# One group of softmax factors for the last two head pairs, and chained products for the first two wide groups

## The chip, the cores and the metric

The kernel runs on one core of one Trainium2 chip. The metric is device microseconds of that core, from the start of the program to its end; lower is better. The engines are PE (TensorE, matmuls), DVE (VectorE), ACT (ScalarE), POOL (GpSimd) and SP (SyncE, which here only issues DMAs). Each engine works through its own list of instructions in order and waits on semaphores of the others.

## The reference

Attention with capped scores feeds a normalized, gated feed-forward layer, and that a second one. Cut to what matters:

```python
# q, k, v: (2, 12, 448, 64)
scores = cap * tanh(q @ k.T / 8 / cap)
attn = exp(scores - max) / (sum(exp(scores - max)) + 1e-09)
x = (attn @ v) -> (896, 768)
# moe: 768 -> 1536 -> 768
xn = x / sqrt(mean(x * x) + 1e-06) * rms_g
x = (silu(xn @ w_gate) * (xn @ w_val)) @ w_out
# moe2: 768 -> 2048 -> 768
h = x @ w_in
out = (max(h, 0) + alpha * min(h, 0)) @ w_out2
```

## The kernel before, in words

**Attention.** There are 12 head pairs (2 batches of 6; a pair is 128 rows of x, two heads of 64). For pair i, `qk` makes the scores in PSUM, `soft` takes tanh and exp on ACT, `pv` multiplies the exponentials with v into the bank `oo`, and `sums` multiplies them with ones to get the row sums (`us`). Divided by the sums, `oo` is x. Every fp32 value that PE multiplies at full speed is split into a high and a low part (names `wh`/`wl` for weights, `xx`, `xh`/`xl` for operands), and a product of two such values takes three matmuls: high by high, low by high, high by low. `sums` works on plain fp32 values, and each of its matmuls writes a quarter of the partitions (32 columns of PE's array): of the eight, four can work side by side.

The quotients are made once for a group of two pairs (`members`): `evac_u` copies the sums out of PSUM on DVE and sends them with two DMAs into a small tile `gt` of 64 partitions by 28; `recip` adds, inverts and splits them into `th` and `tl` (four small DVE instructions) and sends these with two DMAs as rows into `r2`. Later `norm` has PE spread the rows over 128 partitions (`rps`, one matmul) and DVE multiply them with `ee`, the copy of `oo`. All four DMAs are issued by SP. Pair 10 is a group by itself, and the last pair (11) goes another way: `sums_now` makes half-width sums, so that all 128 partitions hold them at once, and `norm_now` inverts them there (ACT, then a DVE reciprocal of 128x448) and multiplies `oo` directly, without DMA.

**The turn to the feed-forward part.** `square` and `rms_sum` (matmuls of squares with ones, L352) give the mean square of batch 1; `rms_root` (ACT) and `rms_tail` (a DVE reciprocal of 128x448) make `rstd` of it; `xnorm` scales x. Until that is there, PE works on products of batch 0, whose `rstd` was made earlier.

**The products.** The gate and value weights are taken in 6 groups g; a pair of weight tiles and the two batches form a 2x2 block product that is computed with seven products P1 to P7 (Strassen's method in Winograd's form) instead of eight. P1 = A11 B11, P2 = A12 B21, P5 = S1 T1, P6 = S2 T2, P7 = S3 T3, P4 = A22 T4, P3 = S4 B22; S and T are sums of weights and of operands. B11 and B21 are the lower and upper three blocks of batch 0; T1, T2 and T3 need batch 1. One product of one group is `product`, 18 matmuls of 448 columns into a pair of PSUM banks. The sums that give the four results are P1+P2, U2 = P1+P6, U2+P7+P5 and U2+P7+P4 and U2+P5+P3.

From group 2 on, P1, P6, P7 and P4 are accumulated one after the other in the same banks (`pa`): between two of them the partial sum is copied out. The first two groups ("early") go another way before the change: P1 starts, is copied (`first_sum`), P2 is added on top of it in the same banks; P6, P7 and P4 are accumulated in other banks (`pb`), and DVE adds P1 to what it reads of them (`u2`, `u3`, `add21`).

**What sets the order.** The program is written in order, engine by engine, without a scheduler; from the first P5 on, PE's work is a list of slots, and a table of hooks (`do(n, rank, ...)`) places the work of the other engines after slot n. A few matmuls are cut in two by hand (`cuts`): `SHORT` cuts the last 64 columns off.

Tiles come from pools with a few buffers; an allocation waits until the former user of the buffer is done. PSUM has eight banks: `ps_s` two pairs, `ps_x` a pair, `ps_o` and `ps_r` a bank each; after attention the pool `pm` takes the place of the last three.

Of the kernel before, what the change touches and what calls it, by code (L numbers as in the profile page):

```python
# [57 lines left out]
def attn_moe_kernel(ctx: ExitStack, tc: tile.TileContext, units, qk_in, v, sel, w, gvec, alpha, out):  # L58
# [206 lines left out]
    members = [[i, i + 1] for i in range(0, NPAIR - 2, 2)] + [[NPAIR - 2]]  # L265
# [8 lines left out]
    def evac_u(i):
# [7 lines left out]
        for k in range(2):  # L282
            nc.sync.dma_start(
# [1065 lines left out]
```

## Time and profile before

| | |
|---|---|
| time, median of 3 runs | 555.68 us (555.52 to 555.75) |
| the profiled execution's own time | 555.48 us |
| its span, first to last instruction | 553.7 us |
| PE busy | 548.4 us, 99% of the span |
| DVE busy | 452.2 us, 82% |
| ACT busy | 366.5 us, 66% |

The time holds the span and some 1.8 us around it (555.48 less 553.7). Shares of busy time are means over the whole program, and PE counts as busy while a matmul is in its pipeline; which engine sets the end of a stage is read from the chain and the timelines.

### The profile page before, as it was taken

What the parts mean: (1) busy time and instruction counts of PE and PEld (TensorE: products, weight loads), DVE (VectorE), ACT (ScalarE), POOL (GpSimd) and SP (SyncE); (2) the same over time, 40 slices, a digit from 0 to 9 for tenths busy, and PEclk for the clock granted to TensorE, in tenths of its full rate; (3) what the DMA queues carried; (4) which work ended last, traced back from release to release, by engine and by line L of the source; (5) the groups of instructions that cost most, each with busy time, mean ns of one, the idle gap of its engine ahead of it and who ended that gap; (6) DMA issues with size and microseconds to landing.
All of it is one profiled execution on the core that took longest, in us unless ns stands there. A gap on an engine that the chain in (4) does not pass through costs nothing.

```text
span 553.7 us, 7698 instructions
## 1 busy us (share of the span) xinstructions
PE 548.4 (99%) x3062; PEld 462.5 (84%) x3062; DVE 452.2 (82%) x514; ACT 366.5 (66%) x427; POOL 100.6 (18%) x54
## 2 busy tenths in 40 slices
PE   8999999999999999999999999999999999999997
PEld 5444544699999999999999999999999999999996
DVE  4797889899998967878898898979866899999242
ACT  7989999458356654586757554787967996467110
POOL 0034762200056431010000038101111000000000
PEclk9999999999999999999999999999999999999999
DMA  7855420400334535065510663005412257013022
GB/s 256 289 173 184 157 77 3 172 2 0 115 117 168 171 115 170 1 217 182 174 54 1 228 225 117 1 0 172 171 58 65 108 203 250 2 59 115 0 101 99
DMA packets 17180, 66.07 MB, mean 119 GB/s; under 512 B 3448, under 2 KB 5368, under 8 KB 17144
## 3 DMA queue, kind: packets, MB, share of 16 engines
q1 hardware_dynamic: 16712, 65.07, 34.3%
q8 instruction: 24, 0.39, 0.3%
q10 hardware_dynamic: 288, 0.38, 0.2%
q0 software_dynamic: 144, 0.13, 0.1%
q14 instruction: 12, 0.10, 0.1%
HBM read 62.66 MB, written 2.75 MB: 118 GB/s over the span
## 4 chain that ended last, share of the span: by engine, by line
PE 98%; ACT 1%; DVE 0%; issue 0%; DVEq 0%
PE m L407 22%; PE s L407 21%; PE m L761 11%; PE s L761 9%; PE s L735 8%; PE m L735 7%; PE oo L234 6%; PE s L205 5%; PE us L247 3%; PE s L420 1%; PE m L420 1%; ACT pt L214 1%; PE warm L431 1%; ACT pt L219 1%; PE us L257 1%; PE rps L330 1%
## 5 line engine op out<-in xcount | busy, mean ns | idle before, releaser
L131 ACT CAST wh<-wt 128x768 fp32r<-128x768 f32 x105 | 87.1, 832 | 69.4 <-PE s L761 25.0
L125 POOL TENSOR_TENSOR wt<-wt 128x768 f32<-128x768 f32 x33 | 77.2, 2348 | 263.6 <-DVE wt L117 133.7
L137 DVE TENSOR_TENSOR wl<-wt,wh 128x768 fp32r<-128x768 f32 x108 | 115.0, 1068 | 11.4 <-ACT wh L131 11.1
L112 ACT CAST top<-raw 128x768 f16<-128x768 bf16 x64 | 68.8, 1078 | 34.1 <-DVE wt L117 20.4
L407 PE MATMUL s<-xx,wh 128*128 128x448 f32 x336 | 81.3, 367 | 0.1
L407 PE MATMUL m<-xx,wh 128*128 128x448 f32 x336 | 80.2, 365 | 0.0
L117 DVE SCALAR_TENSOR_TENSOR wt<-raw,top 128x768 uint32<-128x768 uint32 x68 | 68.6, 1010 | 0.9 <-ACT top L112 0.9
L407 PEld LDWEIGHTS s<-xx,wh 128*128 128x128 f32 x336 | 63.0, 188 | 6.4 <-issue 0.9
L407 PEld LDWEIGHTS m<-xx,wh 128*128 128x128 f32 x336 | 63.1, 188 | 4.9
L625 DVE TENSOR_TENSOR xx<-b,xx 128x896 fp32r<-128x896 f32 (+1 forms) x40 | 48.7, 1226 | 0.6 <-ACT xx L638 0.6
L761 PE MATMUL m<-xx,wh 128*128 128x448 f32 x156 | 47.2, 365 | 0.0
L214 ACT ACTIVATE pt<-s,cinv 128x896 f32<-128x896 f32 (+1 forms) x48 | 41.0, 911 | 5.8 <-PE s L205 5.5
L407 PE MATMUL m<-xx,wl 128*128 128x448 f32 (+1 forms) x170 | 43.3, 364 | 0.0
L407 PE MATMUL s<-xx,wl 128*128 128x448 f32 (+1 forms) x170 | 43.3, 364 | 0.0
L761 PE MATMUL s<-xx,wh 128*128 128x448 f32 x132 | 40.4, 365 | 0.0
L234 PE MATMUL oo<-pt,vt 128*32 128x448 f32 x384 | 38.6, 540 | 0.5 <-ACT pt L219 0.4
L219 ACT ACTIVATE pt<-pt,cap_t 128x3136 f32<-128x3136 f32 (+2 forms) x13 | 35.3, 2713 | 0.4
L735 PE MATMUL m<-xx,wh 128*128 128x448 f32 x120 | 34.1, 365 | 0.0
L407 PEld LDWEIGHTS m<-xx,wl 128*128 128x128 f32 x170 | 31.9, 188 | 2.5
L407 PEld LDWEIGHTS s<-xx,wl 128*128 128x128 f32 x170 | 31.8, 188 | 2.5
L234 PEld LDWEIGHTS oo<-pt,vt 128*32 128x32 f32 x384 | 12.1, 110 | 23.8 <-issue 21.0
L625 DVE TENSOR_TENSOR b<-m,b 128x896 f32<-128x896 f32 (+1 forms) x13 | 11.8, 907 | 24.4 <-PE m L761 18.1
(187 smaller groups left out, 1018.0 us busy)
## 6 DMA issues: line engine op xcount, KB each, us to landing
raw<-w_in SPq DMA_DIRECT2D x68, 768.0 KB
rw<-qk_in SPq DMA_DIRECT2D x11, 480.0 KB
vt<-v_in SPq DMA_DIRECT2D x12, 256.0 KB
out<-b SPq DMA_DIRECT2D x2, 448.0 KB
out<-b SPq DMA_DIRECT2D x2, 224.0 KB
out<-e SPq DMA_DIRECT2D x1, 448.0 KB
out<-c SPq DMA_DIRECT2D x2, 224.0 KB
gt<-us SPq DMA_DIRECT2D x22, 3.5 KB
```

The lines of the kernel that those rows point to most:

```text
L112: copy(top_of[u].bitcast(F16)[:, 1::2], raw_t[u].bitcast(BF16)[:, 4:4 * n + 4:4])
L117: nc.vector.scalar_tensor_tensor(out=f_t[u].bitcast(U32), in0=raw_t.pop(u).bitcast(U32)[:, 1:2 * n + 1:2], scalar=13, in1=top_of.pop(u), o ...
L125: add(out=t, in0=f_t[a], in1=f_t[b], op=op)
L131: copy(h_t[u], f_t[u].rearrange("p (k m) -> p k m", m=P))
L137: nc.vector.tensor_tensor(out=l_t[u], in0=f_t[u].rearrange("p (k m) -> p k m", m=P), in1=h_t[u], op=ALU.subtract)
L214: nc.scalar.activation(out=t[:, 2 * g:2 * g + w], in_=st.pop((i, g))[:, :w, :S], func=AF.Tanh, scale=cinv)
L219: nc.scalar.activation(out=t[:, done:to], in_=t[:, done:to], func=AF.Exp, scale=cap_t)
L234: nc.tensor.matmul(oo[i][q * Q:q * Q + Q, :S], vv[:, n, q % 2 * Q:q % 2 * Q + Q], t[:, min(n, TILES - 1), :], start=c == 0, stop=c == TG, ...
L407: nc.tensor.matmul(ps[:, r, c0:c1], lhs, rhs[:, c0:c1], start=first and n == 0, stop=n == len(mm) - 1, skip_group_check=True,)
L625: nc.vector.tensor_tensor(out=out, in0=a, in1=b, op=op)
L735: nc.tensor.matmul(dst[m], wt[:, kk * MB + m, :], x, start=first and u == 0 and kk == 0 and n == 0, stop=u == 1 and kk == 1 and n == 2, sk ...
L761: nc.tensor.matmul(dst[m], wt[:, kk * MB + m, :], x, start=start and ks + kk == 0 and i == 0, stop=fin and last and kk == 1 and i == 2, sk ...
```

## The change

- **Sums.** All 12 pairs use quarter-width sums and groups of two; pairs 10 and 11 share one group. `sums_now` and `norm_now` are gone: pair 11 gets `evac_u`, a place in `recip`, and a `norm`. The second DMA of the last `evac_u` and of the last `recip` is issued by ACT instead of SP. `oo` of pair 11 is copied by ACT.
- **Squares.** The squares of pairs 10 and 11 are added on DVE (`join_squares`), so that `rms_sum` has two parts instead of three; its result goes to the bank of `ps_o`.
- **Products.** P2 of both early groups comes first and has its own banks (`pb`), then P1 in `pa`; B21 is made before B11. The early groups then use the chain P1, P6, P7, P4 in `pa` as the later groups do; P1, P2, P5, U2 and P4 of group 0 are copied by ACT (`keep_part`, `ps1`), and DVE joins. P4 of group 1 now stands ahead of P1 of group 2. `ps_x` lives on after attention, and `chain_pair` alternates between it and `pm`.
- **Around it.** T3's sum and high part and the high part of S3 of group 0 are made earlier; a silu of one column (`tiny`) draws ACT's table load ahead of T1's casts; weight buffers are assigned in another order; cuts are S/2 and there is one fewer.

The core of the diff:

```diff
     ps_s = ctx.enter_context(tc.tile_pool(name="ps_s", bufs=2, space=PSUM))
+    ps_x = ctx.enter_context(tc.tile_pool(name="ps_x", bufs=1, space=PSUM))
...
-    ps_x = att.enter_context(tc.tile_pool(name="ps_x", bufs=1, space=PSUM))
...
-        h_t[u] = wpool.tile([P, UK, P], F32R, tag="wh", name="wh", bufs=WH)[:, :k]
+        if u not in h_t:
+            h_t[u] = wpool.tile([P, UK, P], F32R, tag="wh", name="wh", bufs=WH)[:, :k]
...
-        us[i] = ps_r.tile([P, 512], F32, tag="u", name="us")
+        us[i] = ps_s.tile([P, 2, 512], F32, tag="s", name="us")[:, 0] if i == NPAIR - 1 else under()
...
-    def sums_now(i):
-        us[i] = ps_s.tile([P, 2, 512], F32, tag="s", name="us")[:, 0]
-        for n, t in enumerate(tiles_of(i)):
-            h = n % 2
-            nc.tensor.matmul(
-                us[i][h * D:h * D + D, :S], half[:, h] if n > 5 else ones[:, :D], t, start=n < 2, stop=n > 5,
-                skip_group_check=True,
-            )
...
-    members = [[i, i + 1] for i in range(0, NPAIR - 2, 2)] + [[NPAIR - 2]]
+    members = [[i, i + 1] for i in range(0, NPAIR, 2)]
...
+    def evac_u(i, queues=(nc.sync, nc.sync)):
...
-        for k in range(2):
-            nc.sync.dma_start(
+        for k, q in enumerate(queues):
+            q.dma_start(
...
-        for r0, x in ((0, th), (32, tl)):
+        for r0, x, q in zip((0, 32), (th, tl), queues):
             row = rr[r0:r0 + w].rearrange("r (p s) -> r p s", p=RP)
-            nc.sync.dma_start(out=row.bitcast(F32), in_=x[m].bitcast(F32))
+            q.dma_start(out=row.bitcast(F32), in_=x[m].bitcast(F32))
...
-    def norm_now(i):
-        b, p = divmod(i, NP)
-        u = sb.tile([P, S], F32, tag="us", name="us")
-        nc.scalar.activation(out=u, in_=us.pop(i)[:, :S], func=AF.Identity, bias=eps_t)
-        for j in (last - 3, last - 2):
-            square(j)
-        nc.vector.reciprocal(out=u, in_=u)
-        nc.vector.tensor_tensor(out=xf[b][:, p, :], in0=oo.pop(i)[:, :S], in1=u, op=ALU.mult)
-        square(i)
+    def join_squares(b):
+        x, y = s2[b].pop(), s2[b].pop()
+        nc.vector.tensor_tensor(out=x, in0=y, in1=x, op=ALU.add)
+        s2[b].append(x)
...
+        for x in ("A12", "A11"):
+            for g in range(2):
+                h_t["g", g, x], l_t["g", g, x] = (
+                    wpool.tile([P, UK, P], F32R, tag=t, name=t, bufs=WH) for t in ("wh", "wl")
+                )
...
-        a(11, xnorm, 0)
-        z(11, xnorm, 1)
+        a(11, xnorm, K3)
+        z(11, xnorm, K3 + 1)
...
-        sums_now(last)
+        sums(last)
+        evac_u(last, (nc.sync, nc.scalar))
+        for j in (last - 3, last - 2):
+            square(j)
         pv(last)
-        xnorm(2)
+        xnorm(K3 + 2)
...
-            pa[g] = pair_tile(ps_s, "s")
-        recip(len(members) - 1)
-        norm_now(last)
+            pb[g] = pair_tile(ps_s, "s")
         late = []
-        product(pa[0], ("g", 0, "A11"), "B11", True, rows=(0,))
+        evac_o(last, nc.scalar.copy)
+        w_lo(("g", 1, "A12"))
+        xnorm(0, late)
+        recip(len(members) - 1, (nc.sync, nc.scalar))
+        xnorm(1, late)
+        xnorm(2, late)
+        lows(late)
+        product(pb[0], ("g", 0, "A12"), "B21", True)
+        w_hi(("g", 0, "S1"))
+        sum4("g", 1)
+        product(pb[1], ("g", 1, "A12"), "B21", True, rows=(0,), span=range(6))
         norm(last - 1, under())
+        norm(last, third()[:, 0])
         square(last - 1)
-        product(pa[0], ("g", 0, "A11"), "B11", True, rows=(1,))
-        for m in range(NP - 3, NP):
-            xnorm(m, late)
-        lows(late)
-        rms_sum(B - 1, third()[:, 0])
+        square(last)
+        join_squares(B - 1)
+        product(pb[1], ("g", 1, "A12"), "B21", True, rows=(0,), span=range(6, 3 * K3))
+        product(pb[1], ("g", 1, "A12"), "B21", True, rows=(1,))
+        rms_sum(B - 1, upper("ms"))
         rms_keep(B - 1)
         rms_root(B - 1)
-        first_sum(0, ct("c21"))
-        w_hi(("g", 0, "S1"))
-        w_lo(("g", 1, "A12"))
-        sum4("g", 1)
+        w_lo(("g", 0, "S1"))
         rms_tail(B - 1)
-        product(pa[1], ("g", 1, "A11"), "B11", True, cuts={(0, 4): (S // 2,), (1, 4): SHORT})
-        first_sum(1, ct("c21"))
-        w_hi(("g", 1, "S1"))
-        c11 = [spare[B - 1][:, :2], xpool.tile([P, 2, S], F32, tag="B22l", name="c11")]
-        product(pa[0], ("g", 0, "A12"), "B21", False)
-        nc.scalar.copy(c11[0], pa[0][:, :, :S])
-        product(pa[1], ("g", 1, "A12"), "B21", False)
...
-        pm = ctx.enter_context(tc.tile_pool(name="pm", bufs=2, space=PSUM))
+        pm = ctx.enter_context(tc.tile_pool(name="pm", bufs=1, space=PSUM))
+        n_chain = [0]
         def chain_pair():
-            return pair_tile(pm, "m")
+            n_chain[0] += 1
+            return pair_tile(*((ps_x, "x") if n_chain[0] % 2 else (pm, "m")))
...
+        d11, ps1 = {}, {}
+        def keep_part(to, g, ps, home):
+            to[g] = home()
+            nc.scalar.copy(to[g], ps[g][:, :, :S])
+        for g in range(2):
+            keep_part(d11, g, pb, lambda: h_of(g)[:, 2:])
+            pa[g] = chain_pair()
+            product(pa[g], ("g", g, "A11"), "B11", True, cuts={} if g else {(0, 4): (S // 2,)})
+        w_hi(("g", 1, "S1"))
+        nc.scalar.activation(out=tiny, in_=cap_t, func=AF.Silu)
         i1 = (B - 1) * NP
         one, low = tile_maker("T1", i1, x0[:, lo3], x1[:, lo3], x0[:, lo3])
         for k in range(K3):
             one(k)
-        nc.scalar.copy(c11[1], pa[1][:, :, :S])
+            if k == 0:
+                w_lo(("g", 1, "S1"))
         for g in range(2):
-            w_lo(("g", g, "S1"))
+            ps1[g] = ct("p1")
+            nc.scalar.copy(ps1[g], pa[g][:, :, :S])
+        for g in range(2):
             w_hi(("g", g, "S2"))
...
-        BANKS = ({"P1": pa, "P2": pa, "P6": pb, "P7": pb, "P4": pb, "P5": pc, "P3": pc},
-                 {"P1": pa, "P6": pa, "P7": pa, "P4": pa, "P2": pb, "P5": pc, "P3": pc})
+        BANK = {"P1": pa, "P6": pa, "P7": pa, "P4": pa, "P2": pb, "P5": pc, "P3": pc}
...
-                product(BANK[p][g], (lay, g, wn), xn, first, cuts={(1, 4): SHORT} if here in PACED else {})
+                product(BANK[p][g], (lay, g, wn), xn, first, cuts={(1, 4): (S // 2,)} if here in PACED else {})
...
-        layer("g", G1, twice(("P5", "P6", "P7", "P3")) + [("P4", 0), ("P1", 2), ("P4", 1)])
+        layer("g", G1, twice(("P5", "P6", "P7", "P3", "P4")) + [("P1", 2)])
...
-            gate(1, g, 0, c11)
-            do(at_["P6"] + 1, 1, u2_first, g, None)
-            soon = g == 1
-            do(at_["P7"] + 1 - soon, 1 + 0.6 * soon, u3, g, lambda: cu("c22"))
-            do(max(at_["P7"], at_["P5"]) + 1 - soon, 1 + 0.6 * soon, add22, g)
-            gate(max(at_["P7"], at_["P5"]) + 2, g, 3, c22)
-            do(at_["P4"] + 1, 1, add21, g)
-            gate(at_["P4"] + 2, g, 2, c21)
-            do(at_["P3"] + 1, 1, add12, g)
+            do(3 + 3 * g, 1.2, join11, g)
+            do(4 + 2 * g, 1.3, silu, g, 0, d11)
+            do(5 + 2 * g, 0.95, times, g, 0, d11)
+            do(3 + g, 0.5, keep_part, c22, g, pc, lambda: cu("c22"))
+            do(at_["P6"] + 1, -1, keep_part, c12, g, pa, lambda g=g: home12(g))
+            do(at_["P7"] + 1, 1, join_part, c22, g, pa)
+            gate(at_["P7"] + 3 - g, g, 3, c22)
+            do(at_["P3"] + 1, 2.2, join_part, c12, g, pc)
             gate(at_["P3"] + 2, g, 1, c12)
+            if g == 0:
+                do(at_["P4"] + 1, -1, keep_part, c21, g, pa, lambda: ct("c21"))
+                gate(at_["P4"] + 1, g, 2, c21)
+            else:
+                gate(at_["P4"] + 1, g, 2, pa)
...
+            w_lo(("g", 0, "S2"))
+            one2(1)
+            w_lo(("g", 1, "S2"))
+            one2(2)
+            w_hi(("g", 0, "S3"))
+            tt(x1[:, lo3], x1[:, hi3], x1[:, lo3], ALU.subtract)
+            operand("T3", x1[:, lo3])
```

Where the instructions stand. PE from the sums of the last pair on, before (L257 `sums_now`, L234 `pv`, L407 `product`, L330 `norm`, L352 `rms_sum`):

```order
L257 MATMUL us<-pt,ones 64x448 x6
L257 MATMUL us<-pt,half 64x448 x2
L234 MATMUL oo<-pt,vt 32x448 x16
L407 MATMUL s<-xx,wh 128x448 x3
L407 MATMUL s<-xx,wl 128x448 x3
L407 MATMUL s<-xx,wh 128x448 x3
L330 MATMUL rps<-r_1_92,sel_t 128x448
L407 MATMUL s<-xx,wh 128x448 x3
L407 MATMUL s<-xx,wl 128x448 x3
L407 MATMUL s<-xx,wh 128x448 x3
L352 MATMUL s<-s_1033,ones 128x448
L352 MATMUL s<-sq,ones 128x448 x2
```

PE at the same place in the changed kernel (L249 `sums`, L236 `pv`, L393 `product`, L322 `norm`, L339 `rms_sum`):

```order
L236 MATMUL oo<-pt,vt 32x448 x16
L393 MATMUL s<-xx,wh 128x448 x3
L393 MATMUL s<-xx,wl 128x448 x3
L393 MATMUL s<-xx,wh 128x448 x6
L393 MATMUL s<-xx,wl 128x448 x3
L393 MATMUL s<-xx,wh 128x448 x6
L393 MATMUL s<-xx,wl 128x448 x3
L322 MATMUL rps<-r_1_93,sel_t 128x448
L322 MATMUL s<-r_1_93,sel_t 128x448
L393 MATMUL s<-xx,wh 128x448 x6
L393 MATMUL s<-xx,wl 128x448 x3
L393 MATMUL s<-xx,wh 128x448 x3
```

The two norms stand behind 24 matmuls of products instead of one norm behind 9; ahead of this piece `sums` has eight matmuls of 32 columns, and the two parts of `rms_sum` follow next. After them only the two P1 (36 matmuls) stand ahead of P5, where 54 stood before.

ACT at the same time, before (from the last exp's follower on: L131 high part of a weight, L578 the root of one column, L337 `norm_now`, L316 `square`, L385 casts of an operand, L359 `rms_root`, L576 `first_sum`):

```order
L131 CAST wh<-wt 128x768
L578 ACT_TABLE_LOAD
L578 ACTIVATE cinv<-rms_b 128x1
L337 ACTIVATE us<-us,eps_t 128x448
L316 ACTIVATE sq<-xf 128x448 x4
L385 CAST xx<-xf 128x448 x3
L359 ACTIVATE spare<-s,rms_b 128x448
L576 COPY c_1222<-s 128x896
L131 CAST wh<-wt 128x768
L576 COPY c_1250<-s 128x896
```

And in the changed kernel (L275 the DMA of `evac_u`, L264 the copy of `oo`, L372 casts, L295 the DMA of `recip`, L346 `rms_root`, L662 `keep_part`):

```order
L275 DMA gt<-us 32x1x28
L308 ACTIVATE sq<-xf 128x448 x2
L567 ACT_TABLE_LOAD
L567 ACTIVATE cinv<-rms_b 128x1
L264 COPY ee<-oo 128x448
L372 CAST xx<-xf 128x448
L295 DMA r_1_93<-tl 4x16x28
L372 CAST xx<-xf 128x448 x2
L133 CAST wh<-wt 128x768
L308 ACTIVATE sq<-xf 128x448 x2
L346 ACTIVATE spare<-ms,rms_b 128x448
L662 COPY b_1264<-s 128x896 x2
```

ACT's queue now holds two DMA issues, each behind a wait for DVE; two squares moved ahead of the table load, and two copies of a product pair stand ahead of T1's casts.

ACT at P6 and P7 of the early groups, in the changed kernel (L629 the high part of an operand, L662 `keep_part`, L133 the high part of a weight):

```order
L133 CAST wh<-wt 128x768
L629 CAST xx<-xf 128x1344
L662 COPY b_1436<-x 128x896
L133 CAST wh<-wt 128x768
L662 COPY c_1440<-s 128x896
L629 CAST xh<-xf 128x1344
L662 COPY b_1436<-m 128x896
L133 CAST wh<-wt 128x768
```

The `b` rows are the copies of U2 out of the chain's banks; P7 of the same group accumulates in these banks and follows them. Before the change, DVE read the banks there (`u2`), and ACT had no copy.

## Rows read from the trace of the kernel before

**Rows 1.** Page, part 1: span and busy time of the engines

```profile
span 553.7 us, 7698 instructions
...
PE 548.4 (99%) x3062; PEld 462.5 (84%) x3062; DVE 452.2 (82%) x514; ACT 366.5 (66%) x427; POOL 100.6 (18%) x54
```

**Rows 2.** All waits of PE for others: total us, times, longest us

```profile
PE warm L431 <- DVE ones L428: 1.1, 1, 1.1
PE oo L234 <- ACT pt L219: 0.4, 1, 0.4
```

**Rows 3.** The chain that ended last, in order of time: start us, length us, what

```profile
90.08 1.64 PE us L247 x16
...
95.12 0.20 PE rps L330
95.32 3.16 PE us L257 x16
...
103.64 0.21 PE rps L330
...
105.69 2.25 PE s L352 x6
107.94 11.04 PE s L407 x56
...
126.29 7.30 PE s L420 x36
...
133.64 7.53 PE s L407 x36
...
239.74 7.38 PE m L407 x37
```

**Rows 4.** Timeline of DVE and ACT: start us, length us, engine, instruction

```profile
91.79 0.62 DVE L280 COPY us<-us 128x448 f32<-128x448 f32 x1
...
95.37 1.28 ACT L578 ACT_TABLE_LOAD   x1
...
96.39 0.68 DVE L376 SCALAR_TENSOR_TENSOR xf<-xf,g_t,spare 128x448 f32<-128x448 f32 x1
...
96.67 0.20 ACT L578 ACTIVATE cinv<-rms_b 128x1 f32<-128x1 f32 x1
...
98.07 0.23 DVE L292 SCALAR_TENSOR_TENSOR gf<-gt,eps_t 32x28 f32<-32x28 f32 x1
...
98.88 0.18 DVE L299 TENSOR_TENSOR tl<-gf,th 32x28 fp32r<-32x28 f32 x1
...
107.81 0.95 DVE L137 TENSOR_TENSOR wl<-wt,wh 128x768 fp32r<-128x768 f32 x1
107.98 0.64 ACT L359 ACTIVATE spare<-s,rms_b 128x448 f32<-128x448 f32 x1 [1.10 <-PE s L352]
...
108.52 0.90 ACT L576 COPY c<-s 128x896 f32<-128x896 f32 x1
108.68 2.94 DVE L362 RECIPROCAL spare<-spare 128x448 f32<-128x448 f32 x1
...
112.45 0.62 DVE L625 TENSOR_TENSOR xf<-xf 128x448 f32<-128x448 f32 x1
```

**Rows 5.** Timeline at the products after attention, the same columns

```profile
128.62 1.31 ACT L638 CAST xx<-xf 128x1344 fp32r<-128x1344 f32 x1
...
132.40 1.09 DVE L625 TENSOR_TENSOR b<-s,c 128x896 f32<-128x896 f32 x1 [0.88 <-PE s L420]
```

**Rows 6.** Timeline of SP's queue, the same columns

```profile
98.91 0.66 SPq L303 DMA_DIRECT2D r<-th  x1
...
100.41 1.30 SPq L101 DMA_DIRECT2D raw<-w_in  x3
```

**Rows 7.** Windows: us, length, busy by engine, clock, DMA share, GB/s

```profile
100.20:100.40 0.20, 0.20 (x8) 0.09 (x4) 0.20 (x1) 0.00 (x0) 0.20 (x1) 1.00 0.13 18
101.20:107.80 6.60, 6.60 (x34) 4.83 (x27) 5.49 (x9) 2.81 (x5) 0.93 (x1) 1.00 0.90 357
```

More of the change, by code (lines that the diff above doesn't have):

```diff
@@ L73, in attn_moe_kernel @@
     cap_t = const.tile([P, 1], F32, name="cap_t")
+    tiny = const.tile([P, 1], F32, name="tiny")
     cinv = aconst.tile([P, 1], F32, name="cinv")
@@ L394, in attn_moe_kernel, with product @@
     fill_ps = {}
-    SHORT = (S - 64,)
-    def product(ps, u, name, first, rows=(0, 1), cuts={}):
+    def product(ps, u, name, first, rows=(0, 1), cuts={}, span=range(3 * K3)):
         wh, wl = h_t[u], l_t[u]
@@ L403, in product @@
             mm = [(a[:, r * K3 + k, :], x[:, k, :]) for a, x in ((wh, xh), (wl, xh), (wh, xl)) for k in range(K3)]
-            for n, (lhs, rhs) in enumerate(mm):
+            for n in span:
+                lhs, rhs = mm[n]
                 edges = [0, *cuts.get((r, n), ()), S]
@@ L410, in product, with products @@
                     )
-    def products(pss, us, name):
+    def products(pss, us, name, first):
         xh, xl = oper[name]
@@ L420, in products @@
                 nc.tensor.matmul(
-                    ps[:, r, :S], wt[u][:, r * K3 + k, :], x[:, k, :], start=n < len(both),
+                    ps[:, r, :S], wt[u][:, r * K3 + k, :], x[:, k, :], start=first and n < len(both),
                     stop=x is xl and k == K3 - 1, skip_group_check=True,
@@ L658, in tile_maker, with h_of @@
             return one, low
+        hb = {}
+        def h_of(g):
+            if g % 2 == 0 and g // 2 not in hb:
+                hb[g // 2] = block(g // 2)
+            return hb[g // 2][:, g % 2 * 4:g % 2 * 4 + 4, :]
+        d11, ps1 = {}, {}
[8 more added lines that the diff above has]
+        nc.scalar.activation(out=tiny, in_=cap_t, func=AF.Silu)
         i1 = (B - 1) * NP
@@ L685, in pslot @@
             early = lay == "g" and g < 2
-            BANK = BANKS[not early]
-            first = p in (("P6", "P5") if early else ("P1", "P2", "P5"))
+            first = p in ("P1", "P2", "P5")
             wn, xn = OPER[p]
@@ L693, in pe @@
                 if first and early:
-                    BANK[p][g] = chain_pair() if p == "P5" else side_pair()
+                    BANK[p][g] = side_pair()
                 elif first and p == "P1":
@@ L702, in pe @@
                     if g == 1:
-                        products([BANK[p][0], BANK[p][1]], [("g", i, wn) for i in range(2)], xn)
+                        products([BANK[p][0], BANK[p][1]], [("g", i, wn) for i in range(2)], xn, first)
                     return
-                product(BANK[p][g], (lay, g, wn), xn, first, cuts={(1, 4): SHORT} if here in PACED else {})
+                product(BANK[p][g], (lay, g, wn), xn, first, cuts={(1, 4): (S // 2,)} if here in PACED else {})
             at_of[lay, g, p] = len(slots)
@@ L829, in attn_moe_kernel @@
                     do(n - 2, 0, lambda u: w_kept(u), u)
-                else:
+                elif u != ("g", 0, "S3"):
                     do(n - 2, 0, w_hi, u)
@@ L886, in attn_moe_kernel @@
             do(0, 6, w_next, u)
-        def h_of(g):
-            if g % 2 == 0 and g // 2 not in hb:
-                hb[g // 2] = block(g // 2)
-            return hb[g // 2][:, g % 2 * 4:g % 2 * 4 + 4, :]
         def vsum(out, ps, b):
             tt(out, ps[:, :, :S], b, ALU.add)
-        def u2(g, home):
-            c12[g] = home()
-            vsum(c12[g], pb[g], c21[g])
-        def u3(g, home):
-            c22[g] = home()
-            vsum(c22[g], pb[g], c21[g])
-        d11 = {}
-        def keep_part(to, g, ps, home):
-            to[g] = home()
-            nc.scalar.copy(to[g], ps[g][:, :, :S])
         def join_part(to, g, ps):
             vsum(to[g], ps[g], to[g])
-        def add22(g):
-            vsum(c22[g], pc[g], c22[g])
-        def add21(g):
-            vsum(c21[g], pb[g], c21[g])
-        def add12(g):
-            vsum(c12[g], pc[g], c12[g])
         def silu(g, q, of):
@@ L974, in second_operands @@
             one2(0)
-            for g in range(2):
-                w_lo(("g", g, "S2"))
-            for k in range(1, K3):
-                one2(k)
+            w_lo(("g", 0, "S2"))
[5 more added lines that the diff above has]
+            operand("T3", x1[:, lo3])
             low2()
```

23 lines of the change are left out of this document (11 added, 12 removed).

## The prediction

> **What bounds the kernel now.** I read the page first: PE is busy for 548.4 of 553.7 us [rows 1]. A busy PE need not be a bound, so the second view is the list of PE's waits for other engines: 1.5 us in all, one at the start and one for the first exp [rows 2]. The third is the chain that ended last; from the first scores to the last store it is nearly all PE's own list of matmuls, and the rows here are those that the change touches [rows 3]. So PE bounds the kernel, and a change can win only what it takes off PE's list or off small gaps that the list of waits doesn't name. DVE and ACT matter where a matmul waits for them, so their timelines are the fourth view, at the turn from attention to the products and at P7 [rows 4, 5]. The sum is made against the profiled execution's 555.48 us; the median of the runs, 555.68, lies 0.2 above it. A difference under 0.2% (1.1 us) I call none.
>
> **What leaves PE's list.** Term 1, the sums of pair 11: the half-width form takes 3.16 us, the quarter-width form of all other pairs 1.64 for the same eight matmuls [rows 3]: -1.5.
>
> Term 2, `rms_sum`: three matmuls of plain fp32 (two records each) take 2.25 us [rows 3], a third of that is 0.75, and one goes: -0.75. In its place DVE adds two squares (0.62, as the subtraction of the same size [rows 4]).
>
> Term 3, one more norm: a `rps` matmul takes 0.2 [rows 3]: +0.2.
>
> Term 4, the cuts: a stretch of 36 matmuls takes 7.30 us (0.203 each), and with one `SHORT` cut, 37 records, 7.38: such a cut costs 0.08 [rows 3]. The stretch of 56 holds 54 matmuls (10.95 us), one `SHORT` and one half cut, and takes 11.04 [rows 3]: the half cut costs 0.01. Four `SHORT` and one half become four halves: -0.3. Nothing else in the number of matmuls changes.
>
> Term 5, a gap at P7: the 36 matmuls that begin at 133.64 take 7.53 instead of 7.30 [rows 3]. P7 adds into the banks of P6, and DVE reads these first, from 132.40 to 133.49 [rows 5], ending 0.15 before P7 starts. After the change ACT copies them instead, in 0.90 [rows 4] against 1.09: of the 0.23 I take -0.2 for group 0. For group 1 the copy stands fifth on ACT (below), from nothing to 0.2 of new wait; I take 0.05, nearer the end at which short overlaps on ACT count.
>
> Sum: -1.5 - 0.75 + 0.2 - 0.3 - 0.2 + 0.05 = -2.5. That makes 553.0 for a profiled execution and 553.2 as a median.
>
> **What must stay hidden for that.** Three chains of other engines end at PE, each with its own cover.
>
> *The factors.* This is the tight one. The sums still start at 95.3 [rows 3]. In the loop DVE's copy starts 1.71 after them (90.08 to 91.79) and takes 0.62 [rows 3, 4]: here it ends at 97.65. Two DMAs go out at once, from SP and ACT. DVE goes on with one `xnorm` of three steps (1.68, from 96.39 to 98.07), a weight's low part (0.95) and another scaling (0.68) [rows 4]: 100.95. The sums have 3.3 to land. From the first step of `recip` to the issue of `th` it takes 0.84 (98.07 to 98.91 [rows 4, 6]), to the end of `tl` 0.99 [rows 4]: issues at 101.8 and about 102.0. The landing isn't in the trace. Below: the packets of the `th` issued at 98.91 run from 100.2 to 100.4 [rows 7], so they are through 1.5 after issue. Above: its partner goes out behind it, after 99.57, and the norm that reads both runs at 103.64 [rows 3], so 4.0 at the most. I take 2.0, near the lower end, since after the packets only the report is left: the factors are there at 104.0. PE comes to the norms with 24 matmuls ahead of them instead of nine. The former norm ran 5.16 after the end of the sums (103.64 less 98.48), so now it is 95.3 + 1.64 + 5.16 + 15 x 0.203 = 105.1. Margin 1.1; at the upper end the factors land at 106.0, and PE waits 0.9.
>
> ACT must be at its second DMA by 102.0. In its queue stand the first DMA (through at about 98.3, with the 0.66 that an issue takes on SP [rows 6]), two squares (0.64 each, as the root of the same size), the table load of 1.28 and the root of one column, 0.20 [rows 4], then the copy of `oo` and one cast of 0.64: 102.3 without any overlap. That is about even with DVE, so `tl` goes out at 102.0 to 102.3. Behind the waiting DMA stand casts that P1 needs, and P1 starts at 109.4.
>
> *The mean square.* From the norms (0.4 for both), 12 matmuls (2.4) and 1.5 of `rms_sum` PE is through at 109.4. DVE's multiplications, ACT's squares and the join, of which `rms_sum`'s second part waits, need some 0.4 + 4 x 0.6 = 2.8 of the first 3.55. Then root to T1: from the start of the root at 107.98 to the end of the first subtraction at 113.07 it is 5.09 [rows 4], plus a cast of at most 0.64: T1's first block at 115.1. P5 stands behind 36 matmuls instead of 54, at 109.4 + 7.3 = 116.7. Margin 1.6, where it was over 5. ACT puts two copies of 0.90, a weight cast (narrower, so at most 0.90), a table load of 1.28 and 0.2 of silu between: 109.4 + 0.64 + 4.2 = 114.2, before DVE's 114.5.
>
> *The copies at P7.* P6 starts at 124.0. Group 0's last matmul is the 30th of 36, so its banks are full at 130.1; before, the reader came as soon (126.29 and 30 x 0.203 is 132.38, and DVE started at 132.40 [rows 3, 5]). ACT then has a copy (0.90), a weight cast (0.90), a copy (0.90), a cast of 1344 columns (1.31 [rows 5]) and group 1's copy (0.90): 135.0, with the 0.15 of the hand-off 135.15. P7 of group 1 is due at 131.3 + 3.65 = 134.95; hence the 0 to 0.2 of term 5.
>
> At nothing I cost: ACT's copies of P1, P5 and P4 and DVE's joins (their banks are used again 7 us later or more; without that cover each would cost its 0.9 to 1.1), T3 and S3 made earlier (behind T2's blocks, ahead of P7 by 2 us), the alternate use of `ps_x` and `pm` (two pairs in turn, as before), and P4 of group 1 ahead of P1 of group 2. DVE loses the reciprocal of `norm_now`, of the size of the 2.94 one [rows 4]. The three raw weight loads stand behind `th` on SP and go out at 102.5 instead of 100.41 [rows 6]; what reads them comes with the later groups, some 25 us on. They matter in another way, as a rival.
>
> **A rule against it.** The row: a table load on ACT starts at 95.37 and takes 1.28, and the root behind it starts at 96.67, 0.02 after its end [rows 4]. The Trainium skill (ScalarE: Activation LUTs, section What ACT_TABLE_LOAD costs) states that a switch of tables costs about 2.66 us, the load and a drain of 1.38. By this rule ACT would come to its second DMA at 103.6, the factors would land at 105.6, and the sum would be 0.5 higher. This trace shows no such drain, so the row decides.
>
> **Rivals.**
> 1. *The factors land late.* The raw loads keep the DMA engines busy from 101.2 to 107.8 [rows 7]; now issued at 102.5 they can run into the `tl` of 102.0 to 102.3. For it: nothing keeps the two apart. Against: `tl` is ahead by a little. At the upper landing of 4.0 PE waits 0.9 to 1.2: 554.2.
> 2. *The slower side: the factors land behind the whole of the three loads.* Issued 2.1 later, the loads would be through at 109.9 [rows 6, 7], and PE would wait 4.8: 558.0. It decides from a landing after 108.7, a wait of 3.6 (556.8). Against it: in the loop such DMAs share the engines with loads, and PE has no wait there [rows 2].
> 3. *ACT is late at P7* by half a microsecond, since its copies stand in order behind a cast that DVE delays: 553.7.
> 4. *T1 late*: the margin of 1.6 used up by a late join or a long ACT queue, and a wait of up to 1: 554.2.
> 5. *The change doesn't do what it says*: the last quarter-width sums don't run side by side; term 1 falls away: 554.7.
> 6. *ACT stops for 1.4 at the table load* ahead of its second DMA, as in the rule above: 553.7.
>
> **How the numbers follow.** Likeliest, 0.66: 553.2, by itself 552.6 to 553.7. Its lower end has no wait at P7, the runs' own 0.2 and some 0.3 for gaps under a tenth that these rows don't resolve. Rival 1: 0.13, of it 0.04 above 554.57, where the difference falls under 0.2%. Rival 2: 0.05. Rival 3: 0.08. Rival 4: 0.04. Rivals 5 and 6: 0.02 each. Faster: 0.66 + 0.09 + 0.08 + 0.04 + 0.02 = 0.89. Within 0.2%: 0.04 + 0.02 = 0.06. Slower: 0.05. The range goes from 552.5 to 554.4, which takes in rivals 3 and 6 and most of 1 and 4.
>
> **What would show it.** Right: a list of PE's waits as short as before; the last sums in 1.6; `rms_sum` in 1.5; P5 at about 116.7 instead of 119.0 (107.94 and 11.04). Wrong: PE idle ahead of the two norms (rivals 1, 2, 6), at P5 (4), at P7 of group 1 (3), or sums of over 2 us (5). The prediction fails if a wait of over a microsecond appears at one of these, or if the later products, which I take as unchanged, gain or lose time.

## The result: 561.68 us, slower by 1.1%

| | before | after |
|---|---|---|
| time, median | 555.71 us (555.52 to 555.75, 4 runs) | 561.68 us (561.38 to 562.89, 4 runs) |
| the profiled execution: time, span | 555.48, 553.7 | 561.83, 560.0 |
| PE busy | 548.4 | 552.5 |

The ratio is 1.0112, 95% interval [1.0095, 1.0130]: 6 us slower, where 553.2 was forecast. The page of the changed kernel, its part 1, beside [rows 1]:

```profile
span 560.0 us, 7686 instructions
...
PE 552.5 (99%) x3060; PEld 461.3 (82%) x3060; DVE 449.3 (80%) x511; ACT 371.0 (66%) x433; POOL 96.3 (17%) x54
```

PE has two records fewer and is busy for 4.1 us more. All its waits for others, beside [rows 2] (total us, times, longest):

```profile
PE rps L322 <- DMA r<-tl: 2.1, 1, 2.1
PE warm L417 <- DVE ones L414: 1.1, 1, 1.1
PE x L393 <- ACT b L662: 0.5, 1, 0.5
PE oo L236 <- ACT pt L221: 0.4, 1, 0.4
```

Two waits are new, 2.6 us together. They don't make 6. The chain that ended last, in order of time (start us, length us, what), beside [rows 3]:

```profile
95.72 1.69 PE us L249 x16
...
100.52 1.57 DVE xf L363
102.09 1.07 DVE gf L284
...
103.54 1.43 DVE th L290
...
104.99 0.18 DVE tl L291
...
105.20 2.23 DMA r<-tl
...
107.56 0.45 PE rps L322
108.01 0.21 PE s L322
...
110.68 1.50 PE ms L339 x4
112.18 3.71 PE x L393 x19
...
119.58 7.39 PE s L406 x36
...
349.47 14.78 PE s L393 x72
```

The reader is to see two things. First, the gains are there: the last sums take 1.69 against 3.16, `rms_sum` 1.50 against 2.25. Between them the chain leaves PE for DVE's factors, whose steps `gf` and `th` take 1.07 and 1.43. In the kernel before, for a half as tall tile, the first took 0.23 [rows 4] and the second 0.17:

```profile
98.68 0.17 DVE L298 CAST th<-gf 32x28 fp32r<-32x28 f32 x1
```

Second, the 36 matmuls of P5 take 7.39 against 7.30 [rows 3]. That is 2.5 ns a matmul, and it doesn't stop there: the 72 from 349.47 on still run at 14.78 / 72 = 0.2053 us each, where 7.30 / 36 is 0.2028. This time from matmul to matmul is called the pace below. From the start of P5 on the trace has 2,130 matmuls: 2,130 x 2.5 ns is 5.3 us, an estimate. No list of waits shows it, since no matmul waits for another engine.

P5 starts at 118.98 before (107.94 and 11.04, [rows 3]) and at 119.58 after, 0.6 later instead of the 2.3 earlier that was forecast. From there to the end of the span it is 434.7 before and 440.4 after, 5.7 more: the pace, and the second wait.

### The profile page after: what moved, and what is told of

Same layout as the page of the kernel before. It is cut to its first block, busy times and chain, and to the rows that moved or that the text cites. A ratio compares the mean times of both kernels' runs of the same rounds, so it can differ in the third digit from the quotient of the medians.

```text
span 560.0 us, 7686 instructions
## 1 busy us (share of the span) xinstructions
PE 552.5 (99%) x3060; PEld 461.3 (82%) x3060; DVE 449.3 (80%) x511; ACT 371.0 (66%) x433; POOL 96.3 (17%) x54
## 4 chain that ended last, share of the span: by engine, by line
PE 91%; DVE 4%; ACT 3%; POOL 1%; issue 1%; DMA 0%; DVEq 0%; POOLq 0%
PE s L393 16%; PE m L393 11%; PE x L393 11%; PE s L772 9%; PE s L746 8%; PE x L772 7%; PE oo L236 6%; PE s L207 6%; PE x L746 4%; PE m L772 4%; PE rps L249 3%; PE m L746 2%; PE s L406 1%; DVE wt L118 1%; DVE wl L139 1%; PE x L406 1%
## 5 line engine op out<-in xcount | busy, mean ns | idle before, releaser
L133 ACT CAST wh<-wt 128x768 fp32r<-128x768 f32 x105 | 87.2, 833 | 69.3 <-PE s L772 24.6
L126 POOL TENSOR_TENSOR wt<-wt 128x768 f32<-128x768 f32 x33 | 72.3, 2197 | 272.5 <-DVE wt L118 98.6
L118 DVE SCALAR_TENSOR_TENSOR wt<-raw,top 128x768 uint32<-128x768 uint32 x68 | 70.4, 1037 | 1.0 <-ACT top L113 1.0
L393 PE MATMUL s<-xx,wh 128*128 128x448 f32 x264 | 64.3, 368 | 0.0
L393 PEld LDWEIGHTS s<-xx,wh 128*128 128x128 f32 x264 | 49.5, 188 | 5.3 <-issue 0.7
L393 PE MATMUL x<-xx,wh 128*128 128x448 f32 x204 | 50.6, 370 | 0.5 <-ACT b L662 0.5
L393 PE MATMUL m<-xx,wh 128*128 128x448 f32 x204 | 50.2, 368 | 0.0
L393 PEld LDWEIGHTS x<-xx,wh 128*128 128x128 f32 x204 | 38.1, 188 | 4.8 <-ACT b L662 0.8
L393 PEld LDWEIGHTS m<-xx,wh 128*128 128x128 f32 x204 | 38.3, 188 | 3.6
L772 PE MATMUL s<-xx,wh 128*128 128x448 f32 x132 | 40.7, 367 | 0.0
L236 PE MATMUL oo<-pt,vt 128*32 128x448 f32 x384 | 38.5, 540 | 0.4 <-ACT pt L221 0.4
L393 PE MATMUL s<-xx,wl 128*128 128x448 f32 x132 | 34.2, 367 | 0.0
L772 PE MATMUL x<-xx,wh 128*128 128x448 f32 x104 | 31.7, 367 | 0.0
L236 PEld LDWEIGHTS oo<-pt,vt 128*32 128x32 f32 x384 | 12.2, 110 | 23.5 <-issue 21.7
L746 PE MATMUL s<-xx,wh 128*128 128x448 f32 x96 | 27.5, 367 | 0.0
L772 PEld LDWEIGHTS s<-xx,wh 128*128 128x128 f32 x132 | 24.8, 188 | 2.3
L393 PEld LDWEIGHTS s<-xx,wl 128*128 128x128 f32 x132 | 24.8, 188 | 2.3
```

Of the source, the lines that this page charges most:

```text
L118: nc.vector.scalar_tensor_tensor(out=f_t[u].bitcast(U32), in0=raw_t.pop(u).bitcast(U32)[:, 1:2 * n + 1:2], scalar=13, in1=top_of.pop(u), o ...
L126: add(out=t, in0=f_t[a], in1=f_t[b], op=op)
L236: nc.tensor.matmul(oo[i][q * Q:q * Q + Q, :S], vv[:, n, q % 2 * Q:q % 2 * Q + Q], t[:, min(n, TILES - 1), :], start=c == 0, stop=c == TG, ...
L393: nc.tensor.matmul(ps[:, r, c0:c1], lhs, rhs[:, c0:c1], start=first and n == 0, stop=n == len(mm) - 1, skip_group_check=True,)
L746: nc.tensor.matmul(dst[m], wt[:, kk * MB + m, :], x, start=first and u == 0 and kk == 0 and n == 0, stop=u == 1 and kk == 1 and n == 2, sk ...
L772: nc.tensor.matmul(dst[m], wt[:, kk * MB + m, :], x, start=start and ks + kk == 0 and i == 0, stop=fin and last and kk == 1 and i == 2, sk ...
```

## The experiments

The theories for the pace were at first the changed cuts (A), chance, in that the stream keeps a pace that any cut or stall can change (A2), and the new order of products and banks (B). Once these had met the first runs, the places of tiles in SBUF came in (E to H). For the late factors, POOL against DVE (C) stood against the DMAs (D). All times are medians; the kernel before ran at 555.67 to 555.83 beside them.

**e1, the cuts of before in the changed kernel.**

```diff
+    SHORT = (S - 64,)
...
-            product(pa[g], ("g", g, "A11"), "B11", True, cuts={} if g else {(0, 4): (S // 2,)})
+            product(pa[g], ("g", g, "A11"), "B11", True, cuts={(1, 4): SHORT} if g else {(0, 4): (S // 2,)})
...
-                product(BANK[p][g], (lay, g, wn), xn, first, cuts={(1, 4): (S // 2,)} if here in PACED else {})
+                product(BANK[p][g], (lay, g, wn), xn, first, cuts={(1, 4): SHORT} if here in PACED else {})
```

> The changed kernel with the cuts of the kernel before: 64 columns cut off (SHORT) at the second product P1 and at the three paced slots, in place of halves. Theory A (the cuts set the pace of the matmul stream, 0.2027 us from matmul to matmul before against 0.2053 after): about 2170 matmuls stand behind the second P1, so 561.8 - 5.8 = 556.0, with a pace of 0.2027. Theory B (the pace comes from the new order of products and banks, and a cut costs only its own 0.08): 562.1, pace 0.2053. In both the wait of 2.1 us ahead of the norms stays.

Measured 561.63 (561.51 to 561.86), pace as in the changed kernel (72 matmuls in 14.78). Theory A falls as the cause of the 6 us.

**e2 and e4, the kernel before with the new cuts, and with none.**

```diff
-        product(pa[1], ("g", 1, "A11"), "B11", True, cuts={(0, 4): (S // 2,), (1, 4): SHORT})
+        product(pa[1], ("g", 1, "A11"), "B11", True, cuts={(0, 4): (S // 2,)})
...
-                product(BANK[p][g], (lay, g, wn), xn, first, cuts={(1, 4): SHORT} if here in PACED else {})
+                product(BANK[p][g], (lay, g, wn), xn, first, cuts={(1, 4): (S // 2,)} if here in PACED else {})
```

(e4 has no `cuts` in either line.)

> The kernel before with the cuts of the changed one: halves at the three paced slots, and no 64-column cut at the second product P1 (its half cut stays). Theory A (a 64-column cut is what brings the fast pace): 555.7 + 5.8 = 561.5, pace 0.2053. Theory A2 (the stream falls into a pace by chance of its phase at any cut or stall and keeps it; the half cut at 108.6 had brought the fast one already): 555.4, pace 0.2027. Theory B (the order of products and banks sets the pace): 555.4 too, pace 0.2027.

> The kernel before without any cut of a matmul. Theory A (cuts bring the fast pace): slow pace 0.2053 from the products on, 561.4. Theory A2 (chance of the phase after any stall): either pace, 555.3 or 561.4, the same one for the whole stream between stalls. Theory B (order and banks): pace 0.2027, 555.3.

Measured 555.50 (ratio 0.9997 [0.9988, 1.0006]) and 555.66 (1.0000 [0.9990, 1.0009]), 72 matmuls in 14.59. So the cuts do not make the difference in pace between the two kernels. (That a cut can change the pace all the same is shown in the last section.) In the times they are worth nothing that these runs resolve; in the rows of e2 a stretch with a half cut takes 7.30 where one with a `SHORT` cut took 7.38 [rows 3]:

```profile
240.00 7.30 PE m L407 x37
```

**e3, the squares later.**

```diff
-        for j in (last - 3, last - 2):
-            square(j)
         pv(last)
...
         recip(len(members) - 1, (nc.sync, nc.scalar))
+        for j in (last - 3, last - 2):
+            square(j)
```

> The changed kernel with the squares of pairs 8 and 9 (ACT), and so POOL's two additions of them, moved behind the last recip. Theory C (POOL's additions and its weight sum, which run from 100.2 to 104.9, slow DVE's scaling and the steps of recip by 3.0 us in sum, and the factors come late by that): recip takes about 0.9 instead of 3.0, th goes out at about 102, the wait of 2.1 at the norms goes, 559.7. Theory D (the factors are late because their two DMAs, or ACT's queue, are slow): the wait stays, 561.8.

Measured 559.55 (559.48 to 559.69): 2.1 less than the changed kernel, as theory C has it. In the changed kernel POOL's timeline (start us, length us) at that place is

```profile
100.21 2.91 POOL L310 TENSOR_TENSOR s<-s,sq 128x448 f32<-128x448 f32 x2 [12.50 <-ACT sq L308]
103.07 1.85 POOL L126 TENSOR_TENSOR wt<-wt 128x768 f32<-128x768 f32 x1
```

and DVE's beside it

```profile
100.52 1.57 DVE L363 SCALAR_TENSOR_TENSOR xf<-xf,g_t,spare 128x448 f32<-128x448 f32 x1
102.02 1.14 DVE L284 SCALAR_TENSOR_TENSOR gf<-gt,eps_t 64x28 f32<-64x28 f32 x1
103.19 0.32 DVE L287 RECIPROCAL gf<-gf 64x28 f32<-64x28 f32 x1
103.54 1.41 DVE L290 CAST th<-gf 64x28 fp32r<-64x28 f32 x1
104.99 0.18 DVE L291 TENSOR_TENSOR tl<-gf,th 64x28 fp32r<-64x28 f32 x1
```

With POOL's additions moved to 103.05, the same rows of DVE in e3 are

```profile
100.03 0.68 DVE L363 SCALAR_TENSOR_TENSOR xf<-xf,g_t,spare 128x448 f32<-128x448 f32 x1
100.63 0.23 DVE L284 SCALAR_TENSOR_TENSOR gf<-gt,eps_t 64x28 f32<-64x28 f32 x1
100.90 0.32 DVE L287 RECIPROCAL gf<-gf 64x28 f32<-64x28 f32 x1
101.25 0.17 DVE L290 CAST th<-gf 64x28 fp32r<-64x28 f32 x1
101.46 0.18 DVE L291 TENSOR_TENSOR tl<-gf,th 64x28 fp32r<-64x28 f32 x1
```

Three steps are stretched, by 0.89, 0.91 and 1.24, in all 3.0, and two of them end just behind an instruction of POOL: `gf` at 103.16 (POOL's second addition at 103.12), `th` at 104.95 (the weight sum at 104.92). e3 moves two squares of ACT as well. That the wait came from POOL and not from ACT's queue is read from this: DVE's steps got longer, not only later, and ACT had done what stands ahead of its DMA by 102.93, while `tl` ended at 105.17. PE has no wait at the norms in e3. The pace stays slow (14.78).

**e5 to e8, tiles moved in SBUF.** No instruction of PE changes in these. e5 puts `tiny` into the tile of `cap_t`, e6 between weights and operands; e7 (the kernel before) and e8 (the changed one) put `eps_t` there:

```diff
-    tiny = const.tile([P, 1], F32, name="tiny")
+    tiny = xpool.tile([P, 1], F32, name="tiny")
```

```diff
-    eps_t = aconst.tile([P, 1], F32, name="eps_t")
+    eps_t = xpool.tile([P, 1], F32, name="eps_t")
```

> The first runs showed the fast pace (0.2027) in every form of the kernel before and the slow one (0.2053) in every form of the changed one, whatever the cuts. What the two differ in besides is where their tiles lie in SBUF: before, weights and operands both begin 32 bytes past a multiple of 64; after, the weights 32 past one and the operands on one. Here the one-column tile of the early silu shares the tile of the cap, which moves everything behind it by 32 bytes: weights 0, operands 32. Theory E (the pace is slow where weights and operands lie differently): slow, 561.8. Theory F (operands 32 past a multiple of 64 are fast by themselves): 561.8 - 5.8 = 556.0. Theory B (the new order of banks and products sets the pace): slow, 561.8.

> The changed kernel with that one-column tile between the weights and the operands in SBUF: weights 0, operands 0 past a multiple of 64. Theory E (same place, fast): 556.0, pace 0.2027. Theory F (operands must be 32 past): slow, 561.8. Theory B: 561.8.

> The kernel before with its one-column tile eps_t between weights and operands in place of its place among the constants of attention: weights 32, operands 0 past a multiple of 64, as in the changed kernel; no instruction differs. Theories E and F: slow pace 0.2053 over some 2190 matmuls, 555.7 + 5.8 = 561.5. Theory B: 555.7.

> The changed kernel with eps_t between weights and operands: weights 32, operands 32 past a multiple of 64, as in the kernel before; no instruction differs. Theories E and F: fast pace 0.2027, 556.0. Theory B: 561.8.

Measured 562.33 (561.60 to 563.09), 559.92 (559.32 to 560.85), 563.64 (563.09 to 564.16; ratio 1.0141 [1.0126, 1.0156]) and 559.84 (559.31 to 560.42). Theory B falls with e7: the old order of products runs slowly too once its operands are moved by 32 bytes. F falls with e5, which should have been fast. E has the sign of e6 to e8 and not the size. So the places, as the allocation of each built program lists them, were laid beside the pace once more, modulo 256 bytes (the table below), and theory G came of it: the distance from the weights to the operands counts. Its rival H gives each pair of places a pace of its own.

**e9 to e12.** The distance in the changed kernel is 96 because three raw buffers of 6176 bytes each with their padding, which stood ahead of the weight buffers (3 x 6176 = 72 x 256 + 96), now stand behind them: a pool lays its buffers out in the order of their first use, and the change makes the weight buffers first. e9 undoes that alone, e10 takes e3's edit with it; e11 gives `eps_t` 128 bytes between weights and operands in the kernel before, e12 moves both by 32 there.

```diff
-        for x in ("A12", "A11"):
-            for g in range(2):
-                h_t["g", g, x], l_t["g", g, x] = (
-                    wpool.tile([P, UK, P], F32R, tag=t, name=t, bufs=WH) for t in ("wh", "wl")
-                )
+        def assign():
+            for x in ("A12", "A11"):
+                for g in range(2):
+                    h_t["g", g, x], l_t["g", g, x] = (
+                        wpool.tile([P, UK, P], F32R, tag=t, name=t, bufs=WH) for t in ("wh", "wl")
+                    )
         for u in conv[:RAW]:
             z(0, w_load, u)
+        z(0, assign)
```

> The last four runs had no change of an instruction's work, and the pace went with the distance in SBUF from the weights to the operands, modulo 256 bytes: 0 (before) 0.2027, 128 (two runs) 0.2040, 96 (the changed kernel and one run) 0.2053, 32 (one run) 0.2067, with a stretch at 0.2045. The distance is 96 in the changed kernel because its weight buffers are allocated ahead of the three raw buffers, of 6176 bytes each, instead of behind them. Here they are allocated behind the first loads again, nothing else: weights and operands both at 128, distance 0. Theory G (the distance modulo 256 sets the pace): 0.2027, 561.8 - 5.8 = 556.0. Theory H (each pair of places has a pace of its own, and operands at 128 are never fast: 0.2040 to 0.2067 so far): 559 to 564. Theory B (order of banks): 561.8.

> The same with the squares of pairs 8 and 9 behind the last recip: both costs undone. Theories G and C: 561.7 - 5.8 - 2.1 = 553.8, under the 555.7 of the kernel before, PE waiting nowhere over 0.6. Theory H: 557 to 562.

> The kernel before with 128 bytes between weights and operands (distance 128), no instruction changed. Theory G: pace 0.2040, 2190 matmuls of 1.33 ns more, 555.7 + 2.9 = 558.6. Theory H: anything from 555.7 to 564.

> The kernel before with weights and operands both moved by 32 bytes (weights 128, operands 128 past a multiple of 256; distance 0), no instruction changed. Theory G: 555.7, pace 0.2027. Theory H: slower, since operands at 128 were slow in two runs.

Measured 557.71 (556.3 to 559.26), 554.59 (0.9981 [0.9972, 0.9990]), 558.86 (1.0057 [1.0043, 1.0071]) and 555.81 (1.0002 [0.9993, 1.0011]). e11 and e12 came out within 0.3 of theory G. H's one firm point, that operands at 128 are never fast, falls with e9, e10 and e12. e9's profiled execution is at 556.3 with the fast pace; its three other runs lie 1.4 to 3 above that, and why is open.

**e13, the other side: the weight buffers first, alone, in the kernel before.**

```diff
-        h_t[u] = wpool.tile([P, UK, P], F32R, tag="wh", name="wh", bufs=WH)[:, :k]
+        if u not in h_t:
+            h_t[u] = wpool.tile([P, UK, P], F32R, tag="wh", name="wh", bufs=WH)[:, :k]
...
+        for x in ("A11", "A12"):
+            for g in range(2):
+                h_t["g", g, x], l_t["g", g, x] = (
+                    wpool.tile([P, UK, P], F32R, tag=t, name=t, bufs=WH) for t in ("wh", "wl")
+                )
         for u in conv[:RAW]:
```

> The kernel before with its weight buffers allocated ahead of the raw buffers, as the change does; every instruction and its order stay. Weights at 0, operands at 96 past a multiple of 256: distance 96. Theory G: pace 0.2053, 555.7 + 5.8 = 561.5. Rival (the pace goes with something else of the change too): 555.7 to 560.

Measured 561.44 (561.19 to 561.79), ratio 1.0100 [1.0086, 1.0115], PE's waits as short as before. The chain of e13 at the products, from P5 on, beside [rows 3] (same matmuls, same order, 7.30 there):

```profile
119.61 7.39 PE m L421 x36
```

The kernels by their places (`time` is the median of all runs of a kernel):

| kernel | weights, operands (modulo 256) | distance | 72 matmuls, us | time |
|---|---|---|---|---|
| before, with e2's cuts | 96, 96 | 0 | 14.59 | 555.50 |
| e12 (before) | 128, 128 | 0 | 14.59 | 555.81 |
| e9 | 128, 128 | 0 | 14.59 | 557.71 |
| e11 (before) | 96, 224 | 128 | 14.69 | 558.86 |
| e6 | 0, 128 | 128 | 14.69 | 559.92 |
| e8 | 32, 160 | 128 | 14.69 | 559.84 |
| changed | 32, 128 | 96 | 14.78 | 561.68 |
| e5 | 0, 96 | 96 | 14.78 | 562.33 |
| e13 (before) | 0, 96 | 96 | 14.78 | 561.44 |
| e7 (before) | 96, 128 | 32 | 14.88 | 563.64 |

The 72 matmuls are those of one place in the program, from the chain of each kernel.

**e14, a copy ahead of two casts.** e10 still has waits that the kernel before has not, the longest of 0.9 at P6 of group 2:

```profile
PE x L393 <- ACT b L664: 0.9, 1, 0.9
...
PE ms L339 <- DVE sq L328: 0.3, 1, 0.3
PE rps L322 <- DMA r<-tl: 0.3, 1, 0.3
```

In the changed kernel ACT's timeline there (start us, length us, and in brackets the idle time ahead) is

```profile
161.83 0.84 ACT L133 CAST wh<-wt 128x768 fp32r<-128x768 f32 x1 [1.14 <-DVE wt L118]
162.57 1.08 ACT L113 CAST top<-raw 128x768 f16<-128x768 bf16 x1
163.52 0.89 ACT L662 COPY b<-x 128x896 f32<-128x896 f32 x1
```

The copy of P1 stands behind a cast that waits for DVE, whose step (2.61 instead of the usual 0.94) again runs beside POOL:

```profile
159.18 2.61 DVE L118 SCALAR_TENSOR_TENSOR wt<-raw,top 128x768 uint32<-128x768 uint32 x1
```

```diff
-                do(at_["P1"] + 1, 0.5, keep_part, d11, g, pa,
+                do(at_["P1"] + 1, -1 if g == 2 else 0.5, keep_part, d11, g, pa,
```

> e10 with ACT's copy of P1 of group 2 moved ahead of the two casts of a weight that stand before it in the same slot. Theory K (PE's wait of 0.9 there is ACT's queue, behind a cast that waits for DVE, which POOL slows): the wait goes, 554.6 - 0.8 = 553.8. Rival (the casts then come late themselves, for a product a few slots on): 554.6, with a wait further on.

Measured 553.33, ratio 0.9961 [0.9949, 0.9973]: faster than both kernels. Five runs lie from 553.16 to 553.43, with a median of 553.25; the sixth, profiled one took 555.69 at a granted clock of 0.95. All its waits of PE:

```profile
PE warm L417 <- DVE ones L414: 1.1, 1, 1.1
PE oo L236 <- ACT pt L221: 0.3, 1, 0.3
```

and two pieces of its chain:

```profile
97.73 1.75 PE us L249 x16
...
119.74 7.30 PE s L406 x36
```

The last sums and P5 both stand 2.1 to 2.2 later than in e10 (95.63 and 117.54), so the time was lost ahead of them, and P5 has the fast pace. The list is therefore good for the wait at P6, which is gone. It does not show that the two waits of 0.3, ahead of P5, are gone in the faster runs.

## Why the prediction was wrong

**The step that failed.** The prediction counted matmuls, found their number unchanged ("Nothing else in the number of matmuls changes") and took the later products "as unchanged". Their number was; their pace was not. The duration of 0.203 came from the kernel before and was carried over as a property of a matmul of 448 columns, when it was one of that matmul and its buffers' places. The list of the change had the cause in plain sight ("weight buffers are assigned in another order") and no price on it, not even a bound. Both of its signs of failing came: a wait of over a microsecond at a place that it names, and later products that lose time. The pace cost some 5.6 us: shown from both sides, by e13 (+5.6 in the kernel before from this alone) and e9 and e10 (the fast pace comes back in the changed kernel).

**The factors.** Rival 1 gave this place 0.9 to 1.2 of wait with raw loads in the way. The place was right, the cause and the size were not: 2.1, from POOL. ACT's two squares were moved ahead of `recip`; before, `recip` was over at 99.06 [rows 4], and POOL's additions came at 99.77. POOL's two additions of them went along, its weight sum came right behind, and so POOL was busy from 100.2 to 104.9, beside DVE's steps of `recip`. The prediction had followed those squares on ACT and not who reads them. Without POOL (e3) the chain behaves as forecast: the last step of `recip` ends at 101.6 (forecast 102.0 for the issue), and the norms run without a wait. The raw loads of rivals 1 and 2 did no harm: the factors' DMA took 2.23 in the chain, near the 2.0 that was taken. One price of the forecast was too low without harm: the first DMA issue on ACT's queue took 1.35 and not SP's 0.66. The Trainium skill (SBUF — State Buffer, section SBUF: two separate sides) says that DVE and GpSimd share a pair of ports under an exclusive lock: a DVE instruction with two inputs in SBUF (if the GpSimd one reads SBUF) or in a two-port mode and a GpSimd instruction block each other, and whichever starts first holds the pair to its end. The trace agrees: `xf` and `gf`, with two inputs, were stretched, `th` took 1.41 instead of 0.17 and ended with POOL's weight sum, and the reciprocal between them, with one input, kept its 0.32 while that sum ran. Whether the cast of `th` ran in such a mode no run shows. Had the order of POOL's instructions been read as that of ACT's was, this rule would have pointed at the wait.

**ACT late at a copy.** Rival 3 expected half a microsecond at P7 of group 1, behind a cast that DVE delays. P7 had no wait at either group. The same mechanism struck elsewhere, at P6 of group 2 (0.5 in the list of waits, 0.9 in e10). e14 lies 1.3 under e10, more than the 0.8 expected. In e10's trace two steps from matmul to matmul at this place take 1.22 and 0.31, where 0.20 is usual: 1.1 more in all, and more than the list names. The last 0.2 is open.

**The terms.** Sums: -1.5 forecast, 3.16 to 1.69 measured. `rms_sum`: -0.75, 2.25 to 1.50. The extra norm: +0.2, 0.21. The cuts: -0.3 forecast; the times of e2 and e4 do not resolve it, and e2's rows bear it out (0.08 a cut). P7 of group 0: -0.2 forecast, and 7.53 [rows 3] became 7.35 in e14:

```profile
134.34 3.70 PE x L393 x18
138.03 3.65 PE m L393 x18
```

Rival 6 did not appear: the table load in the changed kernel runs from 100.54 to 101.82 and the next instruction starts at 101.84. T1 came in time for P5.

So the local terms were right, and with the three costs taken out (e14) the changed kernel runs in 553.3, where 553.2 had been forecast for it. That it meets to 0.1 is partly luck. In e10, P5 stands 21.9 behind the start of the last sums,

```profile
95.63 1.68 PE us L249 x16
...
117.54 7.30 PE s L406 x36
```

where the kernel before has 23.7 (95.32 and 118.98): 1.8 won, not the 2.3 forecast. At least part of the missing half microsecond is `rms_sum`, whose second part waits for DVE's join (the 0.3 above), where the forecast had reckoned time enough (2.8 of 3.55); in e3 and e10 DVE's steps ahead of it run beside POOL's additions, which now stand there. From P5 to the end of the span e14 takes 434.2 where the kernel before takes 434.7.

## What to carry to other kernels

When a kernel is bound by a stream of matmuls, a change in what is allocated, in its size or in the order of first use is an edit of the stream: compare the length of one same stretch of matmuls before and after (here 36 or 72 of them in the chain), not the list of waits, which shows nothing. Take it at more than one place, since the pace can change within a kernel. When work moves on one engine, follow it to its readers on the others, and look at what POOL will run beside DVE's short steps that a DMA waits for.

## What was not expected of the hardware

At the place of the table, the time from matmul to matmul (128 x 128 weights, 448 columns, fp32r, clock granted in full) went with the distance in SBUF from the weights to the moving operands modulo 256 bytes: 202.6 ns at 0, 204.0 at 128, 205.3 at 96, 206.7 at 32 (the 72 above, each divided by 72). The steps are nearly equal, 1.3 to 1.4 ns. All ten kernels of the table fit there. Other distances weren't tried.

The distance isn't the whole rule: at one and the same distance a stall or a cut matmul can change the pace, as theory A2 has it. In e7 (distance 32) PE stalls at P7, at 134.1. The 72 matmuls before the stall have 206.7 ns; behind it the pace is 200.0 up to the cut matmul at 144.4, 204.4 up to the cut at 247.5, and 206.7 from there on. In its chain 7.44 / 36 and 3.72 / 18 are 206.7 ns, and 7.36 / 36 is 204.4:

```profile
127.04 7.44 PE s L420 x36
...
186.14 7.36 PE m L407 x36
...
248.78 3.72 PE s L407 x18
```

In PE's timeline, between the stall and the cut, six matmuls go from 135.80 to 137.00, 200.0 each:

```profile
135.80 1.36 PE L407 MATMUL s<-xx,wh 128*128 128x448 f32 x6
137.00 0.76 PE L407 MATMUL s<-xx,wl 128*128 128x448 f32 x3
```

In e12 (distance 0) it goes the other way: the 46 matmuls between the same stall and the same cut run at 206.7 (six from 135.30 to 136.54), and those around them at 202.7:

```profile
135.30 1.40 PE L407 MATMUL s<-xx,wh 128*128 128x448 f32 x6
136.54 0.78 PE L407 MATMUL s<-xx,wl 128*128 128x448 f32 x3
```

And the changed kernel and e1, whose tiles lie at the same places and which differ in cuts alone, take 14.82 and 14.69 for the same 72 matmuls of the second layer:

```profile
268.23 14.82 PE s L746 x72
```

```profile
268.10 14.69 PE s L748 x72
```

So the places set the pace of most of each stream, and what went before it can set another one. That the new order of the buffers cost the 5.6 us stands without this rule, by e13, e9 and e10. The Trainium skill (SBUF — State Buffer, section SBUF: two separate sides) states that PE never waits for anyone at SBUF. No other engine is in these runs' difference, so the statement on other engines may stand; but PE's own weight loads and moving reads run side by side here, and their places cost up to 2% (14.88 against 14.59). That the two reads hinder each other is argued from this, and no run shows it.
